# Attention, LayerNorm and a two-layer MLP on one core: where the low parts of eight w1 tiles are subtracted

## The chip, the cores and the metric

The kernel runs on one core of one Trainium2 chip, with one launch. The metric is device time in microseconds (us): the time of the whole launch, of which the profiler's span (first instruction to last) is all but a small remainder. The core's engines each work through a queue of their own: TensorE (PE in the profile, its weight loads PEld), VectorE (DVE), ScalarE (ACT), GpSimd (POOL) and SyncE (SP), which here issues the DMA transfers.

## The reference

Four batches, eight heads, 768 tokens, head dimension 64. Attention looks at keys within 16 positions and at one summary per block of 32 keys (keys by their maximum, values by their mean); the result, 3072 tokens of 512 channels, goes through LayerNorm and an MLP with a residual.

```python
k_sum = k.reshape(B, H, nb, block, D).max(axis=3)
v_sum = v.reshape(B, H, nb, block, D).mean(axis=3)
mask_l = np.abs(pos[:, None] - pos[None, :]) < window
scores_s = scale * np.einsum('bhsd,bhnd->bhsn', q, k_sum) + np.log(block)
scores_all = np.concatenate([scores_l_m, scores_s], axis=-1)
a = softmax(scores_all)
x = np.matmul(a, np.concatenate([v, v_sum], axis=2))       # then heads to channels: 3072 x 512
xn = (x - mu) / np.sqrt(var + 1e-06) * g_ln
out = x + np.maximum(xn @ w_ch1, 0.0) @ w_ch2               # w1 512 x 2048, w2 2048 x 512
```

## The kernel before, in words

**Precision.** A matrix product in fp32 is put together from fp16: each operand is split into a high part (the fp16 rounding of the scaled value) and a low part (the scaled value minus the high part, again as fp16), and three products are added up in PSUM: high times high, high times low, low times high. Both MLP weights have to be split in this way before they can be used.

**The way of a weight tile.** w1 and w2 are cut into 16 tiles each, 128x512 elements per tile (`f` = 0 to 15). Each goes through these steps:

- `fetch_w` (L660): one DMA of 512 KB into one of four `raw` buffers; the words come as pairs.
- `merge_w` (L682): three VectorE instructions build the fp32 tile `m` from the two words of each pair.
- `gram` (L692): the squares of the tile are summed, on TensorE for the first three quarters of w1, with a ScalarE Square for the last quarter of w1 and for all of w2.
- `scale_w1` (L718), `scale_w2` (L732): from these sums a power of two is made by which the tiles are scaled: one for each quarter (four tiles) of w1 (with `diag[q]`, the identity times that scale), one chain for all of w2. So no tile of w2 can be split before the last one is merged and summed.
- `split_w` (L749): ScalarE writes the high part, `w[:, 0]` = fp16(scale * m). For w1 the low part is made on TensorE: `diag` times the fp32 tile, plus `minus` (minus the identity) times the high part, both into one PSUM bank (`low`), which ScalarE then copies to `w[:, 1]`. For w2 VectorE makes the low part in one instruction.

The fp32 tile of w1 with number f and that of w2 with number f lie in the same buffer `m{f}`: w2's merge comes after w1's split.

**The MLP.** `g1(s)` (s = 0 to 95) takes 256 tokens and two of the 16 column tiles of w1: 24 matmuls into one of two PSUM banks `h`; ScalarE (relu, high part) and VectorE (low part) empty it. `g2(s)` multiplies the result with w2 for the first three groups of 256 tokens (tiles `a`); the other nine groups use `g2_wide`, a scheme with seven products in place of eight (banks `acc_a`, `acc_s`, `acc_o`). The attention of batch 0 runs ahead of and between these (`s`, `pp`, `o` on TensorE, early), that of the later batches in an fp16 form beside the MLP.

**What sets the order.** `body` does not issue instructions as it goes: it records them in a `Plan`, and `Plan.issue` (L151 to L156) issues them in the order of a compressed table, `ORDER`, a permutation of all recorded operations. Hence nearly every instruction carries line L156, and tiles are told apart by name. Within an engine the issue order is the execution order; waits between engines are added from the data that the instructions read and write. GpSimd shares its queue with small jobs of the LayerNorm (`rs`), copies that lay out keys and values, and later the products with the probabilities (`p<-p,p`) and residual sums (`x<-x,uv`).

Of the kernel before, what the change touches and what calls it, by code (L numbers as in the profile page):

```python
# [54 lines left out]
AT = {4: 16, 5: 19, 6: 23, 7: 24, 8: 26, 9: 30, 10: 33, 11: 37, 12: 41, 13: 46, 14: 51, 15: 54, 16: 60, 17: 63, 18: 67, 19: 71, 20: 76, 21: 79, 22: 84, 23: 87}  # L55

ORDER = (
    "c-lRf3z&^n`^KNOhrx`qA&gUo8AgO?FvuZBq?7Q45|xT{@`*yeN=fAu4ML(Y%Fsa*lW~lki5SPo`A`_lj4}4Q|G&Ne-}Sk!*?Yh5yWX{)bwBrWKlc)6"
# [3 lines left out]
    "yK3&L0)C`Mxf_0qI@?Jw$k!cq&35{>fro-Qta_52=ct<7>6^LJ{-ToHZ%SZ=mipCx@Nb9XX=+t%lPbEpI<9={uOGF_b@9$3tfJM|>-I3~9aTwJO_$wj"
    "-&2RR*NTE~fjbc_<BF>SD2A?L{U$}Zs_tsA5}Drw!h^`cw>CrpaNA{GxxSrEwx;BKHwetJ9{R?567ha*;%PH$uE}=4lI$a%TmrRQwqCvTi#@HKwhc7y"
    "VV<_IqMbFgvC34Wedy-<y^6Io*Vf-*%Pm=ZL8XWqX{sCJH(49@>8yhC$!#6YaHIVmx5BqIZxPy{6kDg)G{M^1T`Emvk=7T6)UZ)DLYr-?TG)dc!Co#}"
    "Cv}3=6JS<^eQf_G*3NDid0T0lHBRf4W%sdyvo2brLR)6FRNIx)V13L^`nx_Fq!jm_U+aSE>DSq#de&W2Hw(bJh1O5)^&j@L-tK1J1>`H*<O8mkzeptQ"
    "T!!w~BgE0w+Gz}|=*Zpst%Jr{U)y1^`r2mrZ{2>d^}25R{5uN$TW1?!<4ix?I$M4FR1?850J>}JCrxG-`)rEM@@v@HQO&R^n(wkS+JESJ>zXfcO_a#}"
# [1046 lines left out]
```

## Time and profile before

| what | value |
|---|---|
| time, median of 3 runs (lowest, highest) | 582.6 us (581.9, 583.89) |
| the profiled execution's own time | 583.74 us |
| its span | 582.0 us |
| PE busy | 571.9 us (98%) |
| DVE busy | 485.7 us (83%) |
| ACT busy | 386.3 us (66%) |
| POOL busy | 113.3 us (19%) |
| granted TensorE clock | 1.00 |

The times are device times of whole launches. The profile was taken in a further launch: its span and its own time differ by 1.74 us, which lie before the first and after the last instruction. Busy time is the time in which an engine executes; its share is an average over a start-up, a middle and a tail. Since every instruction comes from L156, the rows below are read by tile names: `m` a merged weight tile, `low` the PSUM bank of a w1 low part, `w_u` the split w1 tile, `h` and `a` the banks of the two MLP products, `gram` the sums of squares, `scales` the powers of two.

### The profile page before, as it was taken

How to read it: one execution, taken by the hardware profiler on the slowest of the kernel's cores; microseconds unless marked ns; L12 is line 12 of the kernel's file. 1: busy time of each engine (PE TensorE's matmuls, PEld its weight loads, DVE VectorE, ACT ScalarE, POOL GpSimd, SP SyncE). 2: the span in 40 equal slices, each digit the busy share in tenths (PEclk: the TensorE clock that was granted, in tenths of full speed). 3: DMA queues.
4: the chain of work that ended last, by engine and by line, in shares of the span. 5: the costliest groups of instructions: out<-in, count | busy, mean ns of one | idle time of the engine just before them, and what ended most of it. 6: DMA issues, size and time to landing. Idle time of an engine off the chain costs nothing.

```text
span 582.0 us, 16541 instructions
## 1 busy us (share of the span) xinstructions
PE 571.9 (98%) x6440; PEld 464.9 (80%) x6440; DVE 485.7 (83%) x1287; ACT 386.3 (66%) x977; POOL 113.3 (19%) x177
## 2 busy tenths in 40 slices
PE   7999999999999999999999999999999999999997
PEld 5557778875544688888888888888888888888886
DVE  4999999999999999979888798887798776675572
ACT  2899988779566679767777747567665754542440
POOL 6131001012012021231221121131121140020001
PEclk9999999999999999999999999999999999999999
DMA  8898897833557575657547525434335323211010
GB/s 288 253 266 266 298 260 221 218 92 109 128 141 197 115 162 140 130 137 149 153 103 179 135 41 127 113 82 103 97 87 132 82 53 83 65 37 38 1 73 36
DMA packets 107620, 78.40 MB, mean 135 GB/s; under 512 B 68637, under 2 KB 94109, under 8 KB 107542
## 3 DMA queue, kind: packets, MB, share of 16 engines
q1 hardware_dynamic: 107542, 77.36, 52.1%
q8 instruction: 50, 0.82, 0.6%
q14 instruction: 28, 0.23, 0.1%
HBM read 54.77 MB, written 6.29 MB: 105 GB/s over the span
## 4 chain that ended last, share of the span: by engine, by line
PE 88%; DMA 5%; DVE 4%; ACT 1%; SPq 1%; issue 1%; DVEq 0%
PE h L156 41%; PE acc_a L156 12%; PE a L156 11%; PE acc_s L156 9%; PE acc_o L156 8%; DMA raw<-in_w 4%; PE o L156 3%; PE s L156 3%; DVE m L156 2%; PE low L156 2%; DMA bst<-in_ks 1%; SPq L156 1%; DVE x L156 0%; DVE p L156 0%; ACT gram L156 0%
## 5 line engine op out<-in xcount | busy, mean ns | idle before, releaser
L156 PE MATMUL h<-xt,w_u 128*128 128x256 f16 x2304 | 263.7, 273 | 1.0 <-DVE m L156 0.7
L156 PEld LDWEIGHTS <-w_u 128*128 128x128 f16 x2304 | 224.3, 98 | 30.9 <-issue 2.0
L156 PEld LDWEIGHTS <-h_x 128*128 128x128 f16 x1752 | 170.4, 98 | 44.5
L156 DVE TENSOR_TENSOR wide<-wide 128x128 f32<-128x128 f32 (+1 forms) x224 | 75.4, 344 | 28.8 <-ACT wide L156 26.4
L156 DVE TENSOR_TENSOR h_x<-wide,h_x 128x896 f16<-128x896 f32 x72 | 80.0, 1120 | 13.9 <-ACT h_x L156 13.0
L156 ACT CAST h_x<-wide 128x896 f16<-128x896 f32 x72 | 66.8, 932 | 33.2 <-DVE wide L156 33.0
L156 ACT ACTIVATE p<-p,mn 128x120 f32<-128x120 f32 (+1 forms) x192 | 74.1, 387 | 20.6 <-DVE mn L156 20.2
L156 POOL TENSOR_TENSOR p<-p,p 128x480 f16<-128x480 f32 x36 | 41.4, 1152 | 218.6 <-ACT p L156 185.3
L156 ACT ACTIVATE wide<-h 128x512 f32<-128x512 f32 x72 | 42.5, 593 | 61.0 <-PE h L156 44.8
L156 PE MATMUL acc_o<-w,h_x 128*128 128x256 f16 x408 | 56.0, 273 | 0.0
L156 PE MATMUL a<-w,h_x 128*128 128x512 f16 x240 | 53.1, 379 | 0.0
L156 POOL TENSOR_TENSOR x<-x,uv 128x512 f32<-128x512 f32 x18 | 25.8, 1444 | 115.0 <-DVE uv L156 84.6
L156 DVE CUSTOM_DVE_ANT_0 p<-s,mask,sv 128x120 f32<-128x120 f32 x144 | 46.0, 357 | 1.7 <-POOL p L156 1.1
L156 ACT ACTIVATE bst<-bst 128x384 f32<-128x384 f32 (+2 forms) x55 | 32.3, 588 | 20.9 <-DVE vsum L156 10.5
L156 PE MATMUL acc_a<-mix_x,h_x 128*128 128x256 f16 x324 | 44.7, 273 | 0.0
L156 PE MATMUL acc_s<-mix_x,h_x 128*128 128x256 f16 x324 | 43.9, 273 | 0.0
L156 DVE SCALAR_TENSOR_TENSOR m<-raw,m 128x512 uint32<-128x512 uint32 x64 | 42.6, 685 | 0.2
L156 ACT ACTIVATION_READ_ACCUMULATOR p<-p,mn 128x1 f32 x192 | 36.4, 190 | 0.0
L156 PE MATMUL acc_a<-w,h_x 128*128 128x256 f16 x216 | 35.4, 273 | 0.0
L156 POOL TENSOR_TENSOR rs<-mv,mhalf 128x1 f32<-128x1 f32 x24 | 17.2, 717 | 76.7 <-DVE mv L156 66.6
L156 ACT ACTIVATE v<-vst,sv 128x512 f16<-128x512 f32 x36 | 25.6, 714 | 3.7 <-DMA out_x<-x 2.1
L156 DVE SCALAR_TENSOR_TENSOR v<-vst,sv,v 128x512 f16<-128x512 f32 x36 | 26.6, 745 | 0.7 <-ACT v L156 0.7
(137 smaller groups left out, 770.6 us busy)
## 6 DMA issues: line engine op xcount, KB each, us to landing
raw<-in_w SPq DMA_DIRECT2D x32, 512.0 KB
kst<-in_kt SPq DMA_DIRECT2D x36, 184.0 KB
out_x<-x SPq DMA_DIRECT2D x24, 256.0 KB
qs<-in_qt SPq DMA_DIRECT2D x18, 256.0 KB
bst<-in_ks SPq DMA_DIRECT2D x20, 192.0 KB
bst<-in_qa SPq DMA_DIRECT2D x15, 256.0 KB
bst<-in_vs SPq DMA_DIRECT2D x20, 192.0 KB
vst<-in_va SPq DMA_DIRECT2D x36, 96.0 KB
```

Of the source, the lines that this page charges most:

```text
L156: getattr(getattr(nc, engine), op)(*a, **k)
```

## The change

For the eight odd tiles of w1 (`FAR`) the low part is no longer made on TensorE. ScalarE scales the fp32 tile in place, then writes its fp16 rounding as the high part, and GpSimd subtracts the high part from the scaled tile into the low part. The even tiles and w2 are split as before. The constant `PEL` goes, and the table `ORDER` is a new one throughout (one line of each is shown).

```diff
@@ -42,7 +42,7 @@
 WARMV = 4
 RAW, YB, MB = 4, 2, 2
 NQ = 4
-PEL = 16
+FAR = (1, 3, 5, 7, 9, 11, 13, 15)
 SQUARED = 3
 XR, XW1, XW2 = 1, 7, 8
...
-    "c-lRf3z&^n`^KNOhrx`qA&gUo8AgO?FvuZBq?7Q45|xT{@`*yeN=fAu4ML(Y%Fsa*lW~lki5SPo`A`_lj4}4Q|G&Ne-}Sk!*?Yh5yWX{)bwBrWKlc)6"
...
+    "c-k$P37n2q`^T^I7-o!RNQAMA$x<0ZB5Nai$d<i$OX(G%Qpy{Z7Lp24>D4P)QjBWKGDH~6SVPQU#=Z^0jD4Q-`+x80|LN27-0tVT&$*W0a-F%?jw;fk"
...
@@ -754,8 +754,15 @@
             w = place(f"u{f}", "w1", [P, 2, DM], F16)[:]
         else:
             w = work(f"m{(f - MB) % (NF + MB)}", f"w2_{f}", [P, 2, DM], F16)[:]
-        nc.scalar.activation(w[:, 0], x, AF.Copy, scale=sc)
-        if i == 1 and f % 16 < PEL:
+        if i == 1 and f in FAR:
+            nc.scalar.activation(x, x, AF.Copy, scale=sc)
+            nc.scalar.copy(w[:, 0], x)
+            nc.gpsimd.tensor_tensor(w[:, 1], x, w[:, 0], ALU.subtract)
+        else:
+            nc.scalar.activation(w[:, 0], x, AF.Copy, scale=sc)
+        if i == 1 and f in FAR:
+            pass
+        elif i == 1:
             ps = psum("a", f"low{f}", [P, DM])
             with pl.unit():
                 nc.tensor.matmul(ps[:], diag[q][:], x, start=True, stop=False)
```

How the instructions move shows in the order of each engine. On TensorE, in the first quarter of w1, before (`low1` is tile 1's low part in PSUM, `m1_1` its fp32 tile, `w1_u1` its split tile):

```order
L156 MATMUL low1_258<-m1_1_225,diag0_254 128x512
L156 LDWEIGHTS minus_71
L156 MATMUL low1_258<-w1_u1_257,minus_71 128x512
L156 MATMUL low0_256<-m1_0_223,diag0_254 128x512
L156 LDWEIGHTS minus_71
L156 MATMUL low0_256<-w1_u0_255,minus_71 128x512
...
L156 MATMUL low2_260<-m1_2_227,diag0_254 128x512
L156 LDWEIGHTS minus_71
L156 MATMUL low2_260<-w1_u2_259,minus_71 128x512
L156 MATMUL low3_262<-m1_3_229,diag0_254 128x512
L156 LDWEIGHTS minus_71
L156 MATMUL low3_262<-w1_u3_261,minus_71 128x512
```

and now:

```order
L156 MATMUL low2_259<-m1_2_227,diag0_254 128x512
L156 LDWEIGHTS minus_71
L156 MATMUL low2_259<-w1_u2_258,minus_71 128x512
...
L156 MATMUL low0_256<-m1_0_223,diag0_254 128x512
L156 LDWEIGHTS minus_71
L156 MATMUL low0_256<-w1_u0_255,minus_71 128x512
```

The products of tiles 1 and 3 are gone, those of 2 and 0 remain, tile 2 first; the same holds in the other three quarters.

On GpSimd, from the third LayerNorm tile of batch 0 on, before (`rs` is the root of the variance of a token tile, the copies lay out keys, values and masks):

```order
L156 TENSOR_TENSOR rs0_120<-mv0_119,mhalf_66 128x1
L156 TENSOR_TENSOR rs1_142<-mv1_141,mhalf_66 128x1
L156 COPY spare_x10_86<-spare_x10_86 128x2x32
L156 COPY spare_x8_84<-spare_x8_84 128x2x32
L156 COPY spare_x10_86<-spare_x10_86 128x2x32
L156 COPY spare_x9_85<-spare_x9_85 128x2x32
L156 COPY vst0_68<-spare_x5_93 64x512
L156 TENSOR_TENSOR rs2_163<-mv2_162,mhalf_66 128x1
L156 COPY spare_x9_85<-spare_x9_85 128x2x32
L156 COPY emask_64<-msk_96 64x3x24
```

and now, from the first subtraction on:

```order
L156 TENSOR_TENSOR w1_u3_260<-m1_3_229,w1_u3_260 128x512
L156 COPY vst0_68<-spare_x5_93 64x512
L156 TENSOR_TENSOR w1_u1_257<-m1_1_225,w1_u1_257 128x512
L156 TENSOR_TENSOR rs2_163<-mv2_162,mhalf_66 128x1
L156 COPY ksum1_362<-kmax1_358 64x2x24
L156 COPY vst1_69<-spare_x5_93 64x512
L156 TENSOR_TENSOR w1_u5_265<-m1_5_233,w1_u5_265 128x512
L156 COPY spare_x11_87<-spare_x11_87 128x2x32 x2
L156 TENSOR_TENSOR w1_u9_273<-m1_9_241,w1_u9_273 128x512
L156 TENSOR_TENSOR w1_u7_268<-m1_7_237,w1_u7_268 128x512
L156 TENSOR_TENSOR rs3_185<-mv3_184,mhalf_66 128x1
L156 COPY emask_64<-msk_96 64x3x96
```

Subtractions for tiles 3, 1, 5, 9 and 7 stand between the same small jobs; those of 11, 13 and 15 follow a little further on.

On VectorE, at the end of w2's merging and the start of its scales (`m2_14` is a merged w2 tile, `h16_x6` an MLP operand's low part, `kl` and `ql` low parts of keys and queries; the reduction of `scales` starts w2's scale), before:

```order
L156 SCALAR_TENSOR_TENSOR m2_14_322<-raw2_14_321,m2_14_322 128x512
L156 SCALAR_TENSOR_TENSOR h16_x6_430<-h17_433,h16_x6_430 128x512
L156 SCALAR_TENSOR_TENSOR m2_14_322<-raw2_14_321,m2_14_322 128x512
L156 TENSOR_REDUCE kmax2_501<-bst38_506 128x12
L156 SCALAR_TENSOR_TENSOR kl0_345<-kst6_423,sv1_395,kh0_344 128x4x160
L156 SCALAR_TENSOR_TENSOR ql6_422<-qs30_420,sv1_395,qh6_421 128x512
L156 TENSOR_REDUCE scales_72<-scales_72 128x4
L156 SCALAR_TENSOR_TENSOR kl0_345<-ksum1_370,sv1_395,kh0_344 128x4x24
L156 TENSOR_TENSOR scales_72<-scales_72 128x4
L156 SCALAR_TENSOR_TENSOR kl0_345<-ksum1_370,sv1_395,kh0_344 128x4x24
```

and now:

```order
L156 SCALAR_TENSOR_TENSOR m2_14_314<-raw2_14_313,m2_14_314 128x512
L156 SCALAR_TENSOR_TENSOR h16_x6_422<-h17_425,h16_x6_422 128x512
L156 SCALAR_TENSOR_TENSOR m2_14_314<-raw2_14_313,m2_14_314 128x512
L156 SCALAR_TENSOR_TENSOR kl0_337<-ksum1_362,sv1_387,kh0_336 128x4x24
L156 TENSOR_REDUCE kmax2_493<-bst38_498 128x12
L156 SCALAR_TENSOR_TENSOR kl0_337<-kst6_415,sv1_387,kh0_336 128x4x160
L156 SCALAR_TENSOR_TENSOR ql6_414<-qs30_412,sv1_387,qh6_413 128x512
L156 TENSOR_REDUCE scales_72<-scales_72 128x4
L156 SCALAR_TENSOR_TENSOR kl0_337<-ksum1_362,sv1_387,kh0_336 128x4x24
L156 TENSOR_TENSOR scales_72<-scales_72 128x4
L156 TENSOR_SCALAR sv1_387<-sv1_387 128x1
```

The last merge, the key parts and the reduction of `scales` come in the same sequence but for neighbours that changed places.

## Rows read from the trace of the kernel before

**Rows 1.** the page: busy time of the engines; shares of the chain by engine

```profile
PE 571.9 (98%) x6440; PEld 464.9 (80%) x6440; DVE 485.7 (83%) x1287; ACT 386.3 (66%) x977; POOL 113.3 (19%) x177
...
PE 88%; DMA 5%; DVE 4%; ACT 1%; SPq 1%; issue 1%; DVEq 0%
```

**Rows 2.** busy time by stretch: start:end, us, engines' busy us (count), clock, DMA share, GB/s

```profile
0.00:20.00 20.00, 16.30 (x124) 10.94 (x125) 11.91 (x43) 8.39 (x31) 11.99 (x57) 1.00 0.95 302
20.00:50.00 30.00, 28.02 (x334) 19.20 (x333) 28.20 (x108) 26.90 (x87) 6.52 (x14) 1.00 0.91 252
50.00:100.00 50.00, 49.83 (x453) 37.24 (x453) 49.32 (x136) 46.25 (x139) 5.94 (x13) 1.00 0.89 259
100.00:121.00 21.00, 20.31 (x227) 17.84 (x226) 19.99 (x46) 16.55 (x44) 3.14 (x8) 1.00 0.78 193
126.00:578.00 452.00, 452.00 (x5261) 375.05 (x5260) 371.32 (x945) 285.83 (x675) 83.67 (x84) 1.00 0.44 103
```

**Rows 3.** the chain of waits from 30 to 125 us: start, us, what

```profile
74.19 2.15 PE low L156 x6
...
102.04 4.76 DMA bst<-in_ks
...
106.89 0.55 DVE kmax L156
```

**Rows 4.** what VectorE waited for from 0 to 120 us: total, times, longest

```profile
DVE kmax L156 <- DMA spare_x<-in_ks: 6.5, 3, 3.8
DVE p L156 <- PE s L156: 1.2, 1, 1.2
...
DVE scales L156 <- PE gram L156: 0.6, 1, 0.6
```

**Rows 5.** timeline of VectorE at w2's scales: start, us, instruction

```profile
119.60 0.15 DVE L156 TENSOR_REDUCE scales<-scales 128x1 f32<-128x4 f32 x1
```

**Rows 6.** timeline of TensorE at the same place

```profile
120.67 0.38 PE L156 MATMUL gram<-scales,ones 128*128 128x1 f32 x2
...
126.15 0.81 PE L156 MATMUL a<-w,h_y 128*128 128x512 f16 x3
```

**Rows 7.** timeline of TensorE before that place: its one wait; idle time in brackets

```profile
109.33 1.38 PE L156 MATMUL h<-xt,w_u 128*128 128x256 f16 x11 [0.69 <-DVE m L156]
```

**Rows 8.** the tile `low`, its instructions: count, ns min/median/max, first and last start

```profile
L156 PE MATMUL low<-m,diag x32: 592/592/697, 31.0 to 81.1; 128*128 128x512 f32 x32
L156 PE MATMUL low<-w_u,minus x16: 379/379/379, 32.0 to 81.5; 128*128 128x512 f16 x16
L156 ACT CAST w_u<-low x16: 565/586/621, 35.2 to 81.9; 128x512 f16<-128x512 f32 x16
```

**Rows 9.** ScalarE's groups by form: busy us, mean ns

```profile
L156 ACT CAST p<-p 128x480 f16<-128x480 f32 x36 | 21.2, 589 | 0.8
...
L156 ACT ACTIVATE w_u<-m,scales 128x512 f16<-128x512 f32 x16 | 11.0, 719 | 0.1
```

**Rows 10.** GpSimd's groups by form: busy us, mean ns

```profile
L156 POOL TENSOR_TENSOR p<-p,p 128x480 f16<-128x480 f32 x36 | 41.4, 1152 | 218.6 <-ACT p L156 185.3 <-issue 21.1 <-DMA vst<-in_va 8.8
L156 POOL TENSOR_TENSOR x<-x,uv 128x512 f32<-128x512 f32 x18 | 25.8, 1444 | 115.0 <-DVE uv L156 84.6 <-issue 16.1 <-ACT p L156 14.2
```

**Rows 11.** VectorE's groups by form: busy us, mean ns

```profile
L156 DVE TENSOR_TENSOR x<-o,lrc 128x512 f32<-128x512 f32 x18 | 12.4, 688 | 9.9 <-PE o L156 9.4
...
L156 DVE TENSOR_SCALAR lrc<-lsum,sv 128x8 f32<-128x8 f32 x18 | 4.8, 269 | 0.0
```

**Rows 12.** timeline of VectorE at a GpSimd instruction

```profile
143.99 1.07 DVE L156 TENSOR_SCALAR lrc<-lsum,sv 128x8 f32<-128x8 f32 x1
```

**Rows 13.** timeline of GpSimd beside it

```profile
143.75 1.29 POOL L156 TENSOR_TENSOR p<-p,p 128x480 f16<-128x480 f32 x1 [2.70 <-DVE wide L156]
```

**Rows 14.** timeline of VectorE at a later GpSimd instruction

```profile
380.37 0.69 DVE L156 TENSOR_TENSOR x<-o,lrc 128x512 f32<-128x512 f32 x1 [1.20 <-PE o L156]
```

**Rows 15.** timeline of GpSimd beside that

```profile
380.28 1.10 POOL L156 TENSOR_TENSOR p<-p,p 128x480 f16<-128x480 f32 x1
```

More of the change, by code (lines that the diff above doesn't have):

```diff
@@ L62 @@
[L62 to L66, printed above, removed]
@@ new lines @@
+    "RIHt`e4jw}mlbl=wMF;ZHLI#^>dfzj?6#yeLB3X3c{*Vye0w`!_1XW3b#n8<JzT2J`A&91`*e?Ms~vX3x3s6NiY8mCYwBYxSHIg^T1&3o$>3|(O>e7#"
+    "E3Ru+&fN|#RXbPCUDq`q>$Zgt5^t`q>0`a=@_dG#C;zz6h43X+ayxu^s+H>xsTG+Y@eS>~J*ZR_clmy=J#2Stp!GDTZq)ad&gzDm(WwZ#qcwJ~_E-=4"
+    "x>fu21i$~KYN059NgJ($i}k78?HW4eqpX5P*hFp6vo^r?b2m)HLC4oq(|vBOAFK5$ZP#s^yvCAoinY@w>qIqfSUUGcDAo4x%WR9+I_pDqPwO<l6t;#1"
+    "eQl`i)<&OOeQTyIR!;ZXhpxLnZ!NXXwe<IZvLYZU%LZw=<y)GD`y=iFztuJHrR;a>3ZiydG1t&<vW>cBUG%Uva5Y?|>|;9B!n)}VYh_!&ViDKgFDKuJ"
+    "z|0!(bKWBKiJo<L@mrc2St+fxrq)OkT`>^az^c*rje5Xla5u@`@jJ<2tt+GFbQlz@A@Ugeg&MB5i>x}$|IY6z?q9y1O>z(U-(4v^#&fG|trlp3<*Plp"
@@ new lines @@
+    "53u(&(OOs^f5~3AE>s}w?{&wi)pkEg!(G1m>QUZGv9mV7ziJKKVE=|Svs}ANtJF$qcFrPfj$dT=z_eN*F-(1u?KfSwul-9l6o%&d?zYhF@*ioad()@6"
+    "vZ`d`Y^DE~drn!tB#8dNjZ++PU$7W0v%dPlzVvIzVt`)-<MQaiIW4hg6>ZxrR(0$!SB><Y+n^WJNX~Xz0=;?&6m`{BG~l9cs+*E+fwi$0d_UJu9W~F@"
+    "(%-1W4V_mB`-=Prn|vwFbbZxH)7&e5maAnkezyCTt5&*C>3Z0<T8?VkhvYa6wfW7e+6JB0Qh!5VxNS<X5q_>4=968P8mgIwxF+nE?4m7F#ca9_=bl%x"
+    ">*7O};^OrensNa|zUV)35mwg<fsibX^jpa_!XEXGZ1>Zl1Z(5>!JKKXo)x1@+2(y)U3O_o^k>n57WBQHpXTB%(XV!U(YcrX2EJ<xmVw`w{2wM(yyiR8"
+    "p+-UfTw&hIvW@Ie%_{4-j#~>QSra>gBBjB>yRD|Bg2kPhtm*cq`zBnB?x*Q)yH7nr>%-@4zM9)h`juF2a<{lkQoKs?OfUCscyK7mZ_wkqWWC+8a1o2P"
@@ new lines @@
+    "2p4NJ$-l50MCTrY*;U<HpJPL8nZKq1ZiTPms<<rQ0G#v*Eeb#44lB_eK~b*zGE}`eE2nc+lS*akqA%vWqSZPStA%Rq)`#1K*7&DvFP%Q@^Q?sGx_8t|"
+    "-`is#vxdvm05VB{am#&wcTVg4VwBif(@<3{@l8V^I}<)hCeAf+>xid}`nx6GqXNC%rz$URg;gFN)Kiw?LuuhAp})iRT(WN%O7n?U!dCc}F2`@S@;V1="
+    "Qhh~N!_s_BB5fGj7rvvOF5A|JYq<-)K`2Cp=fKTk%C(m0d$JE)>8$1XjqU+(6U`g<hwg;8TS?Uq?MJUiSX*D)d2}>nU0t5G>J-Yk($@|h499`~;QOd`"
+    "cFtFDyWw2A4qHvS`>J1RN3Ag4(8Lznc%Nn4)yY-V>oyXN42M(DyJL1$RqS&xSlx}a3_sJ&(nmUKVIQf_+-6M#pBwdvjq{gnE;>9>eKc2jE>=6K$SZVh"
+    "ou1b^RdyjXag&|$6Wy1@`K--@`wP&R3U0L?vrB$7TA4z>pF;=IP~nQMlHRdlFlHfY*qMIRa~u2+H0Xja=N4!>$Zeue)yxgBh4d<3b=Wmsi}j-&$KU2#"
@@ new lines @@
+    "WB6MNx16mxXhe1U8s}Z3$8C|m(p1+7_sg*0vxnweEn9Du^nv{c$9T~W`2M!t=Ax7(Yyt?`t9hvIE&b(RbMM)^{)YXaOw_s+_Yc^&`hZDeiYDNhQ)~wq"
+    "NW)V;hc6X0)4Wci0|$MQeXs2(^DbtBCEBeItv?Pt!N!3*=^3y%)us|nlEvw&KEyBD*pp~NAJ$lARjjk-Sg!xcMq5vEPr~)3fHS?AEk3v2>dqu^!>_P@"
+    "7Rx%D@s3`qjQWQ)%Fg>yxWFIU!~V;Oy|*n<ly#@Seb~DQ85FWU{61a3*h-zyFg&&-+~~{iKTw5q`$=Eotyf|EyKpF(S?C~@o<wb~@a$nKaT{O!4{r4^"
+    "sNO)-w{XV+*45e(PnI^Kyt24Ze*RL{>V{g?#wF_6c+IjAnjcCDcPFpO_NJb*=_txyygf_P*r%L*O0BA*!0VaZ&g#GV1g(m~hs&_jTurq|t|L&TexdsQ"
+    "E7on`=eY|+dR`4JlBpnBZ9|3pYH%@KxnwucJ^}GB<7Kh-tH$7!dvqvJUOgJR6)w%Hl|%Ewe=s8)bvwdO!HOL!uBxsmz8`IK_?(5`l99bcY$NPPrD&{e"
@@ new lines @@
+    "!PjqV0u@+BPqLYmb}?<{QmyN*I@hgW;ziX(HS1d??*D~1pHY7%kC~cl-?+=+4z?T5-p_1sNH<+g--6!Nu~GDYGPCL+KC9wZv;9;YqYik>)l#}~7nxVF"
+    "UiKaspTxgbx}N?dcyhJ{q~CB)`?Ff*e)21*Oa|+G%+p;0t>wKYc;9$Cq~Fz=te0z>)pAqWeLgjEaP9<M?9M7UsoGJ8H^J~RG8$(qnCVVywwvMKVwHCA"
+    ">bkx|Ki9&Q&$yefk1R!lP=@=N5*FwivY(`pASep&I7KyvXb8x-%GD?M+$4KlyXZ}v{RnPv!{Z2h!3MfaKa0tAJbikR>fEBDm-#Gf$?9V9wwigocfkyi"
+    "1jb^m0yAaEy3x<O++qKP`hu<h*)?kYgpEN{Z>ueNrGT^33OX<!{+`!sFk~Hltm-=YUDRhb_<V);52=eA>+k3lx?CBouHw0PqS(QVHVzl<V{Z^~B{VO&"
+    "pq7z#AFkJysWJ@m($UhZemOl$uuW==_cUha52FsHK=Iu?)q#mH(;w4Hl;md{tt05*3O(e?T2tnd^1OM3S*9V1(gb%pK>x1N-wc@dBt5Ib$)KcVG8NRY"
@@ new lines @@
+    "d+nGG*jVPlmN2M2zOj)>`vf`WD3P5@P_H{gm!Z>s5bViiuclNi(#p`?p>*hb)?CO{VS2J0lwM};?Sa2#F`=Gi9*(ls^gjWVNpDfDfPwQ-?K18<sQ0{a"
+    "4y3M-bImma4%|nrpF!P{?6`l=f|J*H`1WsVkcsj?fnz?1F6R3C-DtGus;1!y?dVN9dG@kI?rdkatE?CB!lP6n6UP}0Q@5atO?AqmG#oZJvPL#d4>C!="
+    "0^X`H*G1W48^)eHEs<%X4$%iEJI4%u2F?784$i@u>eH*|nbF?X3M)-F{-kD^oYb!4REconAf4!B&say^T+hj)3Y~inUiT!22W*N>K*1Nnz5%FXTPq93"
+    "I)l*b%t=Qz!$zuueNV*~s;0~E+3;c#T~BnYeKZ=|*#5xVGr2nHf1!tIoW1stcT4<fioUklR3aT`+QivoKAmzzycg#@rm65^JST}P=B2e%EjWQ@gS5(Y"
+    ">kYk!>*b*(SLjbYFdxYZzv_KXJy-NU7#mARN`t@GnQLEzl`o>SAE1c?^%>7pw7;2Lv(?X*>Q2GcP_P`L79o4I0Nq~yu_uUrE7v193td8?Z}Mw2^GzN*"
```

55 lines of the change are left out of this document (15 added, 40 removed).

## The prediction

> **What bounds the kernel now.** I read the page first: TensorE is busy 98% of the span and holds 88% of the chain that ended last; VectorE has 83% and 4% [rows 1]. Taken alone that says: whatever leaves TensorE comes off the time. These are averages, so the busy time by stretch comes next [rows 2]. It shows two regimes. From 126 to 578 us TensorE is busy for all 452.00 us and VectorE for 371.32: there TensorE alone sets the pace, and nothing of the change lies there. Before 121 us TensorE and VectorE are both nearly full: from 50 to 100 us TensorE has 49.83 and VectorE 49.32 of 50 us; from 20 to 50 us 28.02 and 28.20 of 30; ScalarE has 46.25 in the former, and the DMA engines are at 0.89 to 0.91 of their time. Four resources are close to their limit together. What the change takes away is in this first part: all products of `low` start between 31.0 and 81.5 us [rows 8].
>
> The third view is the place where the regimes meet. w2 can't be split before all of it is merged, by VectorE, and summed; the last reduction of `scales`, which needs both, runs on VectorE at 119.60 us [rows 5], the `gram` product of the scale on TensorE at 120.67, and the first product `a` at 126.15 [rows 6]. I call the start of `a` the pivot. From there on TensorE doesn't stop, so the end is the pivot plus a fixed amount of TensorE work. The question is thus not how much leaves TensorE, but by how much the pivot comes earlier, and the pivot hangs on VectorE's queue as much as on TensorE's.
>
> **What the change removes.** Eight times three instructions on TensorE. The chain shows six of them, two tiles, in 2.15 us [rows 3], 1.08 us a tile: less than the durations of the page's group (two of 592 ns and one of 379 ns a tile, 1.56 us [rows 8]), since matmuls overlap. 8 x 1.08 = 8.6 us of TensorE's time before the pivot. On ScalarE a tile took 719 ns for the high part [rows 9] and 586 ns (the median) for the copy from PSUM [rows 8], 1.31 us; eight, 10.4 us. VectorE loses nothing: the issue order has the same VectorE instructions ahead of the pivot before and after.
>
> **What it adds.** ScalarE now scales in place and casts. The cast from SBUF to fp16 has a near row at 589 ns, and scaling has 719 as one bound and 589 as the other [rows 9]: 1.18 to 1.31 us a tile, so between 1.0 us less in all and nothing. I take nothing: the value nearest the row of the same scaling. GpSimd gets eight subtractions of 128x512. No row shows this form; the nearest are 1152 ns for 128x480 with fp16 output and 1444 ns for 128x512 fp32 [rows 10]. Scaled to 512 columns the first is 1.23 us. I take 1.28, nearer the one with fp16 output: 10.2 us in all, between 9.8 and 11.6. GpSimd has room: it is busy 6.52 of 30 and 5.94 of 50 us [rows 2]. Behind the subtractions in its queue stand `rs` and small copies; an `rs` held by one subtraction comes up to 1.3 us later, and ScalarE's scaling of `x` and the transposes for `g1` wait for it. They are tiles ahead of use, so I put that at zero, with up to 0.7 us as the other end, which is the one wait that TensorE had for such data before the pivot [rows 7]. w2's merge into the buffer of a w1 tile must wait for the subtraction now in place of the `diag` product; in the issue order over 80 operations of all engines lie between the two, so nothing.
>
> **What it costs VectorE.** The price that is not in any list of removed and added work is that of VectorE and GpSimd running at once. At 143.99 us a `lrc` of 8 columns took 1.07 us [rows 12] where the mean of its group is 269 ns [rows 11]; it ended with a GpSimd product that ran from 143.75 for 1.29 us [rows 13]. So VectorE stood still for about 0.8 us. At 380.37 us, on the other hand, an `x<-o,lrc`, which reads PSUM, took its 0.69 us [rows 14] beside a GpSimd product of 1.10 us [rows 15], and the mean of that group is 688 ns [rows 11]: no loss. Which instruction stands beside the subtraction decides, then. The bounds are nothing and the whole of each subtraction, 8 x 1.28 = 10.2 us. In the new order the subtractions of tiles 3, 5 and 15 fall beside softmax and reductions that read PSUM or have one operand, and I count nothing for these; those of 1, 9, 7, 11 and 13 beside runs with one merge or copy among them, which I count at 0.3 us on average, 1.5 us in all.
>
> The Trainium skill ("SBUF — State Buffer", section "SBUF: two separate sides") speaks against this change: it says that VectorE and GpSimd share one pair of ports, which one of them holds as an exclusive lock for a whole instruction when VectorE uses a two-port mode or has two SBUF operands, and the other fully blocks. The pair at 143.99 us agrees, the pair at 380.37 us doesn't contradict it, as one operand lies in PSUM. By the rule alone, with every subtraction beside merges, the sum would be the third rival's below.
>
> **The sum.** TensorE gets 8.6 us of room before the pivot, but VectorE can use only what it now idles. It idles 8.1 us in the first 20 us, 1.8 from 20 to 50, 0.7 from 50 to 100 and 1.0 from 100 to 121 [rows 2]. The first is start-up: 6.5 us of it waits for keys from DMA, and 1.2 for an early product `s` [rows 4]; none of that hangs on `low`. Of the 3.5 us after it, 0.6 waits for TensorE's `gram` [rows 4], 0.6 for a transfer of `bst` (its landing is 4.76 us in the chain, just ahead of `kmax` [rows 3]), and the rest is in small pieces. I let 2.0 of the 3.5 go. At the pivot itself the `gram` product waits in TensorE's queue behind others: the last reduction is over at 119.75 us (119.60 and 0.15) and it starts at 120.67 [rows 5, 6]. With room on TensorE that is 0.9 us. Gains 2.9, stalls 1.5, `rs` 0.2: 1.2 us net. The profiled execution took 583.74 us (a span of 582.0 and 1.74 around it), so it would come to 582.5; it was 1.1 us above the median of the runs, 582.6, and against that the forecast is 581.4 us.
>
> **The rivals.**
>
> (a) TensorE's saving pays. If TensorE, not VectorE, sets the pivot, the time falls by up to 8.6 us, to 574.0; if half of it goes through (all 3.5 us of VectorE's idle time, 0.9 at the pivot, no stalls, and some of the start), 578. For it: the chain of waits runs over `low` itself [rows 3]. Against it: VectorE has 0.7 us of idle time in 50 us there, and its work isn't less.
>
> (b) The end on the other side: VectorE is blocked. If a subtraction falls beside merges (the instructions that write `m` have their operands in SBUF, `raw` and `m`), each costs the 0.7 to 1.28 us of a held instruction: 5.6 to 10.2 us. Less the 2.9 us of gains that is 2.7 to 7.3 us slower, 585.3 to 589.9; I take 586. It decides from 0.36 us a subtraction on, where stalls reach 2.9 us. For it: the held `lrc`. Against it: at the places where the new order puts them, most neighbours read PSUM.
>
> (c) Nothing comes of it: the transfers (0.89 of the DMA engines' time from 50 to 100 us) or the start-up set when w2's last tile is merged, and the time saved on TensorE becomes waiting: 582.6. For it: the landing in the chain at 102.04 us [rows 3]; against it, that VectorE waits 0.6 us in 21 there.
>
> **How the numbers follow.** I count less than 0.3% as no change: 580.85 to 584.35 us. The forecast's case, with gains and stalls each off by a us or so (579.6 to 583.4), has a chance of 0.50, of which 0.16 lies below 580.85. Rival (a) has 0.18, all of it faster; (b) 0.22, of which 0.20 is slower; (c) 0.10, of which 0.07 is no change, 0.02 faster and 0.01 slower. That makes faster 0.36, no change 0.43, slower 0.21. The range from 577.4 to 585.2 leaves out the better half of (a) and half of (b), about 0.19.
>
> **What would show it.** Right: `a` starts at about 125 us in place of 126.15, and the way from it to the end is the same; VectorE stays over 98% busy from 50 to 100 us while TensorE now shows idle time there of some 5 to 7 us, ended by VectorE (`h_x`, `m`, `xn`); few VectorE instructions beside the eight subtractions are longer than their groups' means. Wrong on one side: no new idle time of TensorE before 121 us, and the pivot at 118 to 122 us. Wrong on the other: merges of 1.3 to 2 us in place of their usual time beside subtractions, and the pivot past 128 us. A pivot that moves while the end doesn't, or the reverse, would make the fixed remainder wrong, and with it the whole way of adding up.

## The result and the profile after

The changed kernel takes 587.0 us (median of 6 runs, 586.65 to 587.59) where the kernel before takes 582.86 us (6 runs beside it, 581.9 to 583.89). The ratio is 1.0072, with a 95% interval from 1.0058 to 1.0086: 4.1 us slower. The forecast was 581.4 us, 577.4 to 585.2.

The page of the changed kernel, busy time and shares of the chain, answers to [rows 1]:

```profile
PE 568.7 (97%) x6416; PEld 463.1 (79%) x6416; DVE 494.0 (84%) x1287; ACT 386.8 (66%) x977; POOL 130.2 (22%) x185
...
PE 86%; DVE 10%; ACT 2%; DMA 1%; issue 1%; POOL 1%; POOLq 0%
```

TensorE gave up 3 us of busy time, not 8.6; part of the rest is time at a lower clock, shown below. VectorE took 8 us more for the same 1287 instructions. Of these 8 us, 5.5 lie behind the pivot (377.5 us against 372.0), where the run e3 below, in the same new order and without subtractions, has them too (377.7) and they cost nothing. In the chain VectorE rises from 4% to 10%.

Busy time by stretch, to be held against [rows 2]:

```profile
0.00:20.00 20.00, 15.73 (x121) 10.65 (x122) 11.66 (x44) 7.72 (x28) 12.14 (x56) 1.00 0.93 298
20.00:50.00 30.00, 27.38 (x313) 17.94 (x312) 29.10 (x108) 26.76 (x89) 8.55 (x19) 1.00 0.84 247
50.00:100.00 50.00, 44.27 (x410) 33.96 (x409) 46.90 (x125) 43.17 (x128) 14.48 (x17) 0.93 0.84 251
100.00:121.00 21.00, 20.17 (x195) 17.70 (x194) 20.61 (x44) 18.10 (x50) 3.81 (x6) 1.00 0.74 197
130.00:578.00 448.00, 448.00 (x5225) 371.51 (x5223) 374.48 (x935) 284.77 (x673) 86.14 (x82) 1.00 0.44 104
```

From 130 to 578 us TensorE is busy for all 448.00 us, as it was for all 452.00 from 126 us before. The loss lies ahead of that. From 50 to 100 us TensorE now idles 5.7 us (44.27 busy, 49.83 before), but VectorE idles too, 3.1 us against 0.7, and TensorE's granted clock is 0.93.

TensorE at the pivot, against [rows 6]:

```profile
124.36 0.38 PE L156 MATMUL gram<-scales,ones 128*128 128x1 f32 x2
...
129.84 1.46 PE L156 MATMUL a<-w,h_y 128*128 128x512 f16 x6
```

The first `a` starts at 129.84 us, 3.69 us later. From there to the end of the span it is 455.86 us (585.7 less 129.84); before it was 455.85 (582.0 less 126.15). So the whole difference of the two profiled spans, 3.7 us, lies before the pivot.

**VectorE is held.** VectorE at three of the eight subtractions:

```profile
42.49 1.14 DVE L156 TENSOR_SCALAR rc<-sum 128x4 f32<-128x4 f32 x1
...
61.54 0.92 DVE L156 TENSOR_SCALAR m<-raw 128x512 uint32<-128x512 uint32 x1
...
66.45 1.64 DVE L156 SCALAR_TENSOR_TENSOR x<-xn,rs,x 128x512 f16<-128x512 f32 x1
```

GpSimd beside it (`w_u<-m,w_u` is the subtraction; the second row holds those of tiles 9 and 7, the last two are those of tiles 13 and 15):

```profile
41.98 1.62 POOL L156 TENSOR_TENSOR w_u<-m,w_u 128x512 f16<-128x512 f32 x1 [5.49 <-ACT w_u L156]
...
59.90 2.27 POOL L156 TENSOR_TENSOR w_u<-m,w_u 128x512 f16<-128x512 f32 x2 [3.91 <-ACT w_u L156]
...
66.02 1.53 POOL L156 TENSOR_TENSOR w_u<-m,w_u 128x512 f16<-128x512 f32 x1 [2.69 <-ACT w_u L156]
75.87 3.36 POOL L156 TENSOR_TENSOR w_u<-m,w_u 128x512 f16<-128x512 f32 x1 [8.32 <-ACT w_u L156]
81.81 1.16 POOL L156 TENSOR_TENSOR w_u<-m,w_u 128x512 f16<-128x512 f32 x1 [2.59 <-DVE m L156]
```

The division's `rc<-sum`, four columns, ran for 1.14 us and ended with the subtraction (41.98 and 1.62 make 43.60). VectorE's groups by form say what is usual:

```profile
L156 DVE SCALAR_TENSOR_TENSOR x<-xn,rs,x 128x512 f16<-128x512 f32 x24 | 18.9, 792 | 3.8 <-ACT x L156 3.8
...
L156 DVE TENSOR_SCALAR m<-raw 128x512 uint32<-128x512 uint32 x32 | 14.1, 447 | 1.1 <-DMA raw<-in_w 1.1
...
L156 DVE TENSOR_SCALAR rc<-sum 128x4 f32<-128x4 f32 x12 | 3.1, 255 | 0.0
```

Means are 255, 447 and 792 ns with the held ones in them; the medians are 0.16, 0.42 and 0.74 us. The excess, an instruction's time less the median of its group, is 0.98, 0.50 and 0.90 us, 2.4 us in all. It goes the other way too: at 75.87 us the subtraction of tile 13 took 3.36 us in place of 1.16, beside five `m` instructions of VectorE that follow each other from 75.39 to 78.21 us:

```profile
75.39 1.29 DVE L156 SCALAR_TENSOR_TENSOR m<-raw,m 128x512 uint32<-128x512 uint32 x2
76.59 0.42 DVE L156 TENSOR_SCALAR m<-raw 128x512 uint32<-128x512 uint32 x1
76.93 1.28 DVE L156 SCALAR_TENSOR_TENSOR m<-raw,m 128x512 uint32<-128x512 uint32 x2
```

It ended at 79.23 us, 1.0 us after the last of them. For a subtraction's result, on the other hand, no instruction of TensorE, VectorE or ScalarE waited.

**TensorE then waits, and its clock falls.** The chain of waits over the third hold, and TensorE's row there, with its idle time in brackets:

```profile
66.54 1.56 DVE x L156
68.10 0.60 DVE m L156
68.70 0.61 DVE h_y L156
...
69.36 2.74 PE h L156 x12
```

```profile
69.36 1.03 PE L156 MATMUL h<-xt,w_u 128*128 128x256 f16 x4 [3.47 <-DVE h_y L156]
```

The held `x` (1.56 us of the chain) delays `h_y`, which frees a bank of `h`, and TensorE stands for 3.47 us. The holds at 61.54 and 66.45 us can account for 1.4 of these; in e3, without subtractions, TensorE waits for `h_y` at that place for 1.35 us. In the stretches after it, its clock (the 1.00 and 0.50 ahead of the DMA share) is at half:

```profile
66.00:68.00 2.00, 0.00 (x0) 0.00 (x0) 2.00 (x2) 2.00 (x9) 1.53 (x1) 1.00 0.77 262
68.00:70.00 2.00, 0.65 (x4) 0.46 (x5) 2.00 (x6) 1.51 (x5) 0.00 (x0) 0.52 0.92 281
70.00:72.00 2.00, 2.00 (x11) 1.50 (x10) 1.46 (x4) 1.36 (x5) 0.00 (x0) 0.50 1.00 276
72.00:74.00 2.00, 2.00 (x12) 1.74 (x11) 0.76 (x5) 1.01 (x3) 0.00 (x0) 0.50 1.07 121
```

The granted clock is 0.50 to 0.52 where it was 1.00, that is the lower of its two levels, 1.2 in place of 2.4 GHz, so twelve products of `h` took 2.74 us of the chain; in the chain of the kernel before twelve take 1.31:

```profile
57.34 1.31 PE h L156 x12
```

### The profile page after: what moved, and what is told of

Its sections match the earlier page's. It is cut to its first block, busy times and chain, and to the rows that moved or that the text cites. A ratio compares the mean times of both kernels' runs of the same rounds, so it can differ in the third digit from the quotient of the medians.

```text
span 585.7 us, 16476 instructions
## 1 busy us (share of the span) xinstructions
PE 568.7 (97%) x6416; PEld 463.1 (79%) x6416; DVE 494.0 (84%) x1287; ACT 386.8 (66%) x977; POOL 130.2 (22%) x185
## 4 chain that ended last, share of the span: by engine, by line
PE 86%; DVE 10%; ACT 2%; DMA 1%; issue 1%; POOL 1%; POOLq 0%
PE h L156 37%; PE acc_a L156 12%; PE a L156 11%; PE acc_s L156 9%; PE acc_o L156 8%; DVE m L156 4%; PE o L156 3%; PE s L156 3%; PE v L156 1%; DVE h_x L156 1%; PE warm L156 1%; DVE x L156 1%; DVE vsum L156 1%; DMA bst<-in_ks 1%; DVE p L156 1%; ACT w_u L156 1%
## 5 line engine op out<-in xcount | busy, mean ns | idle before, releaser
L156 PE MATMUL h<-xt,w_u 128*128 128x256 f16 x2304 | 266.6, 274 | 4.3 <-DVE h_y L156 3.5
L156 DVE TENSOR_TENSOR wide<-wide 128x128 f32<-128x128 f32 (+1 forms) x224 | 78.1, 363 | 22.6 <-ACT wide L156 20.4
L156 POOL TENSOR_TENSOR p<-p,p 128x480 f16<-128x480 f32 x36 | 44.9, 1250 | 172.7 <-ACT p L156 119.4
L156 POOL TENSOR_TENSOR x<-x,uv 128x512 f32<-128x512 f32 x18 | 27.5, 1538 | 151.6 <-DVE uv L156 128.1
L156 DVE CUSTOM_DVE_ANT_0 p<-s,mask,sv 128x120 f32<-128x120 f32 x144 | 44.8, 333 | 3.4 <-POOL p L156 3.4
L156 DVE SCALAR_TENSOR_TENSOR v<-vst,sv,v 128x512 f16<-128x512 f32 x36 | 28.5, 797 | 0.3
```

Of the source, the lines that this page charges most:

```text
L156: getattr(getattr(nc, engine), op)(*a, **k)
```

## The experiments

Three theories stood after the trace was read: VectorE held by subtractions, TensorE's fallen clock, and the new order itself. Each run is given as ratio to the kernel before on the same chip; the medians of before on these chips lay between 582.8 and 583.2 us.

**The order (e1).** The new split with the table `ORDER` of before.

> The new split (eight odd tiles scaled and cast by ScalarE, subtracted by GpSimd) in the issue order of before: each subtraction stands where ScalarE copied the low part from PSUM. Three theories. Held: GpSimd's subtractions hold VectorE (three instructions were 1.05, 0.50 and 0.90 us longer than usual in the changed kernel, 2.4 us). Clock: the room on TensorE lets it idle for 3.5 us, its granted clock falls to 0.5, and products at half speed make VectorE wait 2.4 us. Order: the new issue order costs by itself. Held expects slower than before by 1 to 5 us here (584 to 588), other instructions being beside the subtractions; Clock about 586, if TensorE idles over 3 us at a stretch, else 583; Order expects before's time or less, 580 to 583.

Measured: 587.23 us, ratio 1.0074 (1.0057 to 1.0091), the same as the changed kernel. The excess of held instructions, counted as above, is 5.7 us over eight, 3.3 more than in the changed kernel, at the same time: held time doesn't simply add up to lost time. The new order is not the cause, and it is no cure either.

**The other half of that pair (e2).** The new order with all sixteen low parts on TensorE.

```diff
+SPLIT = ((2, 0, 3, 1), (6, 4, 5, 7), (8, 10, 9, 11), (12, 14, 13, 15))
+BEHIND = {5: 6, 7: 6, 9: "l10", 11: 10, 13: 12, 15: 14}
...
```

> All sixteen low parts by TensorE as before, in the new issue order (the products of an odd tile at or a little after the place of its cast, its copy from PSUM behind them). Order expects 586 to 588, as the changed kernel. Held and Clock both expect before's time within 1.5 us, 582 to 584: no subtraction, and no room on TensorE.

Measured: 596.63 us, 1.0236 (1.0213 to 1.026), worse than any theory had it. The PSUM banks forced me to put six of the eight odd tiles' products behind other tiles' copies, so this mixes the order with my placing. It decides nothing; e1 answers the question.

**No subtractions (e3).** The writes in `early` are issued ahead of all else; the empty GpSimd operation keeps the numbering of `ORDER`.

```diff
-            nc.gpsimd.tensor_tensor(w[:, 1], x, w[:, 0], ALU.subtract)
+            pl.early.append(lambda v=w: tc.nc.vector.memset(v[:, 1], 0.0))
+            pl.ops.append(("gpsimd", []))
...
```

> The changed kernel without the eight subtractions (low parts of the odd tiles are zeros that VectorE writes at the very start, where it waits for data; the output misses them). Held expects the 2.4 us back and, with VectorE no longer late, part of its waits too: 582 to 584.5, first product a at 125.5 to 127.5 us in place of 129.84. Clock expects little if TensorE still idles over 3 us in a row: 586 to 587; Order 586 to 587.

Measured: 583.97 us, 1.0019 (1.0001 to 1.0037). Against the changed kernel's 1.0072 the eight subtractions cost 0.53%, 3.1 us. TensorE at its pivot:

```profile
120.60 0.38 PE L159 MATMUL gram<-scales,ones 128*128 128x1 f32 x2
...
126.26 0.81 PE L159 MATMUL a<-w,h_y 128*128 128x512 f16 x3
```

126.26 us, where before it was 126.15 [rows 6]: with nothing held, and 8.6 us less to do, TensorE is no earlier. Its room became idle time, as the busy times show (20 to 121 us):

```profile
20.00:50.00 30.00, 27.91 (x312) 18.96 (x311) 28.53 (x108) 26.96 (x89) 6.21 (x17) 0.94 0.86 241
50.00:100.00 50.00, 46.48 (x461) 36.23 (x460) 48.74 (x130) 45.77 (x138) 6.34 (x11) 1.00 0.85 261
100.00:121.00 21.00, 19.71 (x219) 17.11 (x217) 20.13 (x49) 17.57 (x47) 4.08 (x7) 1.00 0.69 183
```

**The clock (e4).** Products of no use fill the place where TensorE idled.

```diff
+                for c in range(32 if s == 3 and u == 1 else 0):
+                    nc.tensor.matmul(ps[:, u, :], wt["w1h", f][:, c % 4, :], xh[:, :, c % 4, :], start=True, stop=True)
```

> The changed kernel with 32 extra products (about 3.5 us) on TensorE ahead of the fourth h tile's second half, overwritten by the real ones: TensorE is busy where it idled from 65.9 to 69.4 us. Clock expects the granted clock at 1.00 throughout, the two waits of VectorE for TensorE (1.7 and 0.7 us) gone and 584.5 to 585.5. Held expects no change, 586.5 to 587.5, as the three held instructions remain; Order the same, 587.

Measured: 587.28 us, 1.0083 (1.0062 to 1.0105). In the profiled execution the clock stayed at 1.00, and the pivot, with a span of 584.8 us, came 0.87 us earlier:

```profile
60.00:80.00 20.00, 19.32 (x189) 15.23 (x187) 19.11 (x51) 18.51 (x52) 8.99 (x7) 1.00 0.86 261
```

```profile
128.97 2.32 PE L156 MATMUL a<-w,h_y 128*128 128x512 f16 x10
```

The medians show no gain. Of the six executions three have a mean clock of 1.00 and a median of 586.6 us; the other three have 0.997 and 589.1 us, so the filling didn't always keep the clock. Yet at full clock the kernel is still 3.8 us above the 582.8 of before on this chip, and 3.5 above e3's executions at full clock (583.1, table below): the loss doesn't need the fallen clock, and the theory that the clock carries it fell. What VectorE no longer waited for TensorE (3.0 us from 20 to 122 us in the changed kernel, 0.6 here) it waited for transfers instead (2.8 us, 0.8 in the changed kernel).

**Only some subtractions (e8).** Those of tiles 3, 7 and 11, beside which VectorE was held, left out.

```diff
-            nc.gpsimd.tensor_tensor(w[:, 1], x, w[:, 0], ALU.subtract)
+            if f in (3, 7, 11):
+                pl.early.append(lambda v=w: tc.nc.vector.memset(v[:, 1], 0.0))
+                pl.ops.append(("gpsimd", []))
+            else:
+                nc.gpsimd.tensor_tensor(w[:, 1], x, w[:, 0], ALU.subtract)
```

> The changed kernel without the subtractions of tiles 3, 7 and 11 (their low parts are zeros), beside which VectorE was held; those of 1, 5, 9, 13 and 15 stay. If the three held instructions are the cost: 583.5 to 584.5, as without any subtraction. If each subtraction costs alike: 586 (three eighths of 3 us back).

Measured: 586.07 us, 1.0051 (1.0033 to 1.0068): 0.32% above e3, to which the narrow form of the theory had it equal, so that form fell. It is the 586 us of an equal cost for each subtraction, though the interval overlaps that of the changed kernel. The trace says why: with three subtractions gone, others fell beside VectorE instructions that can be held.

```profile
43.46 1.12 DVE L159 TENSOR_SCALAR rc<-sum 128x4 f32<-128x4 f32 x1
...
74.85 2.27 DVE L159 SCALAR_TENSOR_TENSOR m<-raw,m 128x512 uint32<-128x512 uint32 x2
```

These are beside the subtractions of tiles 1 and 13, where VectorE was not held in the changed kernel; `rc` has an excess of 0.96 us and the first of the two `m` one of 0.99. Which instruction is hit is chance of a few tenths of a microsecond; that some are is not.

**Twice the subtractions (e12).** Each issued twice in a row.

```diff
-            nc.gpsimd.tensor_tensor(w[:, 1], x, w[:, 0], ALU.subtract)
+            with pl.unit():
+                for _ in range(2):
+                    nc.gpsimd.tensor_tensor(w[:, 1], x, w[:, 0], ALU.subtract)
```

> The changed kernel with each of the eight subtractions issued twice in a row on GpSimd. If what GpSimd's subtractions do beside VectorE is the cost (3.0 us for eight, changed kernel against the one without subtractions): about 590, between 588.5 and 592. If their number doesn't matter: 586.5 to 587.5.

Measured: 592.66 us, 1.0169 (1.0152 to 1.0186), 0.97% or 5.7 us above the changed kernel. VectorE and GpSimd in the worst stretch:

```profile
62.27 4.76 DVE L156 SCALAR_TENSOR_TENSOR m<-raw,m 128x512 uint32<-128x512 uint32 x3
...
69.00 1.64 DVE L156 SCALAR_TENSOR_TENSOR x<-xn,rs,x 128x512 f16<-128x512 f32 x1
70.56 1.64 DVE L156 SCALAR_TENSOR_TENSOR m<-raw,m 128x512 uint32<-128x512 uint32 x1
```

```profile
60.88 5.60 POOL L156 TENSOR_TENSOR w_u<-m,w_u 128x512 f16<-128x512 f32 x4 [2.63 <-ACT w_u L156]
...
68.56 3.08 POOL L156 TENSOR_TENSOR w_u<-m,w_u 128x512 f16<-128x512 f32 x2 [0.75 <-ACT w_u L156]
```

Three `m` instructions in a row took 4.76 us in place of some 2.0. The excess over all held instructions, eleven of them, is 8.3 us, 5.9 more than in the changed kernel, near the 5.7 us that the kernel loses. In e1 the two were not near each other, and here TensorE also waited once, 0.8 us, for a doubled subtraction; so the size of the match is in part luck. That the loss grows with the number of subtractions is not: 1.0019 with none (e3), 1.0051 with five (e8), 1.0072 with eight, 1.0169 with sixteen.

**Where the gain went (e5, e6, e7, e9, e10, e11, e13, e14).** All keep the order of before, but that e13 and e14 exchange the places of two fetches. They take work away before the pivot, alone and together: TensorE (the odd tiles' products and nothing in their place; e5 and e7 keep the changed kernel's two ScalarE instructions, scaling in place and casting), VectorE (the last merge instruction of the odd w2 tiles), ScalarE (one instruction per odd w1 tile), transfers (eight of w2's sixteen).

```diff
 # VectorE: merge_w, of the kernel before (e6), of the split without subtractions (e7, e11, e14)
-        nc.vector.scalar_tensor_tensor(x, lw, 29, x, ALU.logical_shift_right, ALU.bitwise_or)
+        if i == 2 and f % 2:
+            pl.ops.append(("vector", []))
+        else:
+            nc.vector.scalar_tensor_tensor(x, lw, 29, x, ALU.logical_shift_right, ALU.bitwise_or)
...
 # ScalarE: split_w, odd tiles of w1, against e5 (e10, e11, e14); e9 leaves out nc.scalar.copy(w[:, 1], ps[:]) instead
-            nc.scalar.activation(x, x, AF.Copy, scale=sc)
-            nc.scalar.copy(w[:, 0], x)
+            nc.scalar.activation(w[:, 0], x, AF.Copy, scale=sc)
+            pl.ops.append(("scalar", []))
...
 # transfers: fetch_w and, the last two lines, issue (e13, e14)
+SHARE = {3: 0, 2: 1, 7: 4, 11: 5, 8: 6, 15: 9, 12: 10, 14: 13}
+        if i == 2 and f in SHARE:
+            raw[f, i] = raw[SHARE[f], i]
+            pl.ops.append(("sync", []))
+            return
...
+        a, b = (order.index(self.fetch[f, 2]) for f in (4, 7))
+        order[a], order[b] = order[b], order[a]
```

> The issue order of before, the products of the eight odd tiles gone from TensorE, nothing in their place (ScalarE scales and casts; the low parts are zeros written by VectorE at the very start; the output misses them). It shows what the room on TensorE, 8.6 us, is worth by itself. If VectorE sets the pivot: 581.5 to 583.5, no gain. If TensorE sets it: 574 to 578. As the prediction had it (2.9 us of gains): 580.

> The kernel before, with the last of the three merge instructions left out for the eight odd tiles of w2 (it adds the three lowest bits of a weight): 8 x 0.6 = 4.8 us less on VectorE before the pivot, TensorE as it was. If VectorE alone sets the pivot: 577.5 to 579. If TensorE and VectorE are both at their limit, so that neither gains alone: 581 to 583.

> Both at once: the products of the odd tiles gone from TensorE as in the run of the order of before without subtractions, and 4.8 us of merges gone from VectorE. If VectorE alone sets the pivot: the same as with fewer merges alone, 577.5 to 579. If both engines are at their limit: 577 to 578.5 here while each alone shows under 1.5 us. If a third (ScalarE or the transfers) holds the pivot: 581 to 583 in all three.

> The kernel before without ScalarE's copies of the eight odd tiles' low parts from PSUM (the products stay, the low parts are zeros written by VectorE at the very start): 8 x 0.59 = 4.7 us less on ScalarE before the pivot, TensorE and VectorE as before. If ScalarE alone holds the pivot (it is at 92% from 50 to 100 us, while less work on TensorE, on VectorE or on both gave nothing): 578 to 579.5. If the engines hold each other, each alone gaining nothing: 581.5 to 583.5.

> Order of before, the products of the odd tiles gone from TensorE and one ScalarE instruction fewer for each of them (high part at once, no scaling in place, low parts zeros): TensorE 8.6 and ScalarE about 4.9 us less, VectorE full. If TensorE and ScalarE are the pair that holds the pivot: 577 to 579. If VectorE with its full queue holds it: 582 to 584.

> All three relieved: as the run with less on TensorE and ScalarE, and the last merge instruction of the eight odd w2 tiles left out too (VectorE 4.8 us less). If the three engines hold each other: 576 to 579 here, while each alone and each pair gives under 2 us. If something else holds the pivot (transfers, the place of the h products in the order): 581 to 583 again.

> The kernel before with eight of the sixteen transfers of w2 left out (pairs of tiles are merged from one raw tile, so half of w2 has the other half's values): 4.2 MB less, 32 raw transfers become 24. If the transfers alone hold the pivot: 576 to 580. If the resources hold each other, each alone gaining nothing: 581.5 to 583.5.

> TensorE, VectorE and ScalarE relieved as in the run with less on all three, and the eight transfers of w2 left out too. If the transfers are the fourth that holds the pivot: 575 to 579. If not, and what holds it is a chain of latencies in the first 80 us, or the place of the h products in the order: 581 to 583, as without.

| run | less work on | ratio (95%) |
|---|---|---|
| e5 | TensorE 8.6 us | 1.0021 (1.0007 to 1.0035) |
| e6 | VectorE 4.8 us | 0.9999 (0.9986 to 1.0013) |
| e9 | ScalarE 4.7 us | 0.9997 (0.9986 to 1.0009) |
| e13 | transfers, 4.2 MB | 0.9996 (0.9984 to 1.0008) |
| e7 | TensorE, VectorE | 1.0003 (0.9989 to 1.0017) |
| e10 | TensorE, ScalarE | 0.9997 (0.9981 to 1.0012) |
| e11 | TensorE, VectorE, ScalarE | 0.9993 (0.9977 to 1.0009) |
| e14 | all four | 0.9957 (0.9941 to 0.9973) |

None alone gains anything, and e5 costs 0.2%. That is not the bare relief of TensorE: e10, where ScalarE writes the high part at once and has one instruction less, costs nothing. With all four relieved the gain is 0.43%, 2.5 us. So no single engine sets the pivot: VectorE, to which my sum gave that part, does not either.

The executions of one run differ in TensorE's mean granted clock, and mostly the time goes with it. Median us by that clock (executions):

| run | 0.999 to 1.00 | 0.996 to 0.997 | 0.994 |
|---|---|---|---|
| e3 | 583.1 (6) | 584.4 (4) | 586.4 (2) |
| e4 | 586.6 (3) | 589.1 (3) | |
| e7 | 583.2 (4) | 582.6 (6) | |
| e11 | 581.6 (4) | 583.0 (5) | 584.2 (2) |
| e14 | 580.1 (4) | 581.1 (6) | |

Two further executions of e7, at 0.990 and 0.991, have 584.6. The kernel before, e6, e9 and e13, which leave TensorE its work, are at 0.999 or 1.00 in every execution. So room on TensorE comes with lower clocks, and in e11 and e14 a part of the gain, some 1 us, is missing where the clock is lower. A fallen clock can make an execution long, and a long wait of TensorE can be what the clock fell after; the table does not say which. With fewer merges (e6) TensorE shows what comes next:

```profile
50.00:100.00 50.00, 50.00 (x454) 37.40 (x455) 46.19 (x130) 46.18 (x140) 5.97 (x14) 1.00 0.90 261
100.00:121.00 21.00, 21.00 (x235) 18.68 (x234) 19.24 (x46) 16.47 (x44) 2.77 (x8) 1.00 0.75 196
```

It is full for all 71 us. And where TensorE is relieved, the place of its work matters. The kernel before, then e14:

```profile
30.00:80.00 50.00, 48.46 (x467) 33.28 (x464) 48.31 (x154) 47.70 (x144) 9.52 (x21) 1.00 0.96 275
80.00:120.00 40.00, 39.31 (x388) 33.75 (x388) 39.00 (x91) 33.38 (x97) 4.83 (x11) 1.00 0.80 210
```

```profile
30.00:80.00 50.00, 44.27 (x440) 31.53 (x432) 47.16 (x152) 44.80 (x140) 10.97 (x22) 0.97 0.85 236
80.00:120.00 40.00, 39.95 (x435) 35.00 (x435) 37.16 (x94) 32.93 (x95) 5.03 (x11) 1.00 0.58 158
```

The removed products all lay between 31 and 82 us [rows 8]. There TensorE idled 1.5 us before and 5.7 us in e14, 4.2 of the 8.6 us gone into waiting, and its clock was at 0.97. From 80 us on it is full in e14, 39.95 of 40 us, with the products that the order of before has there. What it waited for up to 80 us, in e14, the three largest:

```profile
PE s L164 <- ACT x L164: 1.6, 1, 1.6
PE s L164 <- ACT pT L164: 1.5, 2, 0.8
PE pp L164 <- ACT p L164: 1.2, 2, 0.7
```

These are steps of the early attention, from TensorE through VectorE to ScalarE and back. I read them as latencies of a chain that none of the four reliefs shortens; that reading was not tested by itself. That the order of the `h` products, drawn for a busier TensorE, could be drawn anew to use the room is left open: no run tried that, and the changed kernel's new table did not do it.

## Why the prediction was wrong

- **The view held.** The pivot, fixed time behind it: right, 455.86 against 455.85 us.
- **TensorE's room turns to idle time.** Right in kind. The size, 5.7 us from 50 to 100 us with 5 to 7 forecast, was luck: 3.5 of it is the one wait at 65.89 us, made longer by held instructions; with nothing held (e3) it is 3.5 us in all.
- **"Gains 2.9".** This is the first step that failed. Two terms, "I let 2.0 of the 3.5 go" and 0.9 us at the pivot, together are measured as nothing: with the new order and without subtractions 1.0019 (e3), with the order of before 1.0021 (e5). The 3.5 us were misread, too. Between "0.6 for a transfer" and "small pieces" I passed over rows of the same view, of VectorE before:

```profile
DVE m L156 <- DMA raw<-in_w: 1.1, 2, 0.6
DVE kmax L156 <- DMA bst<-in_ks: 0.8, 2, 0.6
```

So 1.9 us waited for transfers and 0.6 for TensorE's `gram` [rows 4]; with all the small pieces at most 1.6 us, not 2.0, could hang on TensorE. I had taken the engine with the least idle time but one for the limit, and its idle time for the gain; e6 shows that 4.8 us less on VectorE gain nothing either. A gain of 0.9 us in `gram`'s queue needs everything ahead of it earlier, and the last `h` products, from 80 us on, were not.
- **"Stalls 1.5".** The second. It was 3.1 us (changed kernel against e3), 2.4 of it seen directly in three instructions. I gave nothing to the subtraction of tile 3, by what stood beside it in the issue order; it was the worst, 0.98 us. Places of two engines in an issue order don't say what will run side by side: a few tenths decide it, as e8 shows. A size per subtraction would have served: 3.1 us over eight is 0.39 us, and e12's next eight cost 0.71 us each. The row of the held `lrc` [rows 12] had 0.8 us.
- **"`rs` 0.2" and ScalarE at nothing.** One weight load of TensorE waits 0.3 us for `rs`, which none did before: no more than was allowed for. ScalarE's busy time is 386.8 us against 386.3 [rows 1], as forecast; whether the high part, now ready one instruction later, costs something is open (e5 against e10).
- **VectorE over 98% busy from 50 to 100 us** was wrong: 94% (46.90). It waited 1.7 us for `gram` while TensorE ran at half clock, but with the clock full there (e4) it is 95%, 47.59 of 50 us.
- **Rival (b)** was the mechanism: VectorE blocked, 586 forecast, with a chance of 0.22. Its 3.4 us came near the measured 4.1 by luck: stalls of at least 5.6 us less gains of 2.9, where the runs showed 3.1 less nothing. (The sentence on the skill's rule calls it the third rival; it is the second.) That leaves about 1 us of the 4.1 that e3 and e5 show as well: no subtraction, 0.2% slower. In e3 it goes with the clock: the six executions at full clock have 583.1 us, 0.3 above before, the six others 583.8 to 587.1. Why the clock falls, and whether it is the cause or what follows a late execution, is open; in e3's profiled execution it was at 0.83 from 40 to 50 us, with no single idle time of TensorE above 0.8 us from 20 to 50 us.
- **Rivals (a) and (c).** (a) is refuted: TensorE relieved gains nothing (e5, e10). (c), given 0.10, says what became of TensorE's room, waiting, but not why: without a quarter of the weight transfers alone nothing changes (e13); with the three engines relieved as well they count (e11 0.9993, e14 0.9957).

The Trainium skill's rule, "SBUF — State Buffer", section "SBUF: two separate sides", that of a GpSimd instruction and a VectorE instruction in a two-port mode or with two SBUF inputs whichever starts first keeps the shared ports for its whole instruction and the other fully blocks, is borne out one way: a four-column VectorE instruction, which with its one SBUF input falls under the rule only in a two-port mode, waited 0.98 us for a subtraction. The other way the wait was longer than one instruction: the subtraction at 75.87 us came to its end only 1.0 us after the last of five merge instructions in a row, four of which had started after it.

No version beats the kernel before: the pieces of this change that cost nothing also gain nothing, and e14, which is faster, leaves out work.

## What to carry to other kernels

Where several engines, and the transfers, are each some 90% busy in a stretch, take work from one in a trial that puts nothing in its place, before building the exchange: here that trial shows no gain at all. Count what lands beside a full VectorE on GpSimd by its number, not by the neighbours in an issue order: here each instruction of 1.2 us cost the kernel some 0.4 to 0.7 us. And ask of room on an engine where in time it lies: before 80 us TensorE only waited longer.

## What the runs showed of the hardware

- A VectorE instruction of four columns with one operand from SBUF was held for 0.98 us by a GpSimd subtraction; one with a PSUM operand, `h_y<-h` at 59.83 us, took its usual 0.69 us beside the two subtractions from 59.90 us:

```profile
59.83 0.69 DVE L156 SCALAR_TENSOR_TENSOR h_y<-h,h_y 128x512 f16<-128x512 f32 x1
```

- GpSimd's 128x512 subtraction, fp32 less fp16 into fp16, took 1.16 us undisturbed, under the 1.28 I took, and 3.36 us beside five merges in a row (3.26 in e4, at 74.21 us).
- After TensorE had idled 3.47 us its granted clock was at 0.50 to 0.52 from 68 to 74 us, although it was busy from 69.36 us on. In e4's profiled execution, with products of no use in that place, it was 1.00 from 60 to 80 us; in e3's it was at 0.83 from 40 to 50 us, where TensorE was busy for 9.62 us, after 8.29 of the 10 us before.
